# A list-scheduled attention, token mixer and gated unit: first scores without fillers ahead, leads and delays by kind of step, angles of batch 0 from group 20

## The chip, the cores and the metric

The kernel runs on one core of one Trainium2 chip. The metric is the device time of one execution in microseconds (us). Before the change the median of three runs is 404.01 us (402.75, 404.01 and 409.04).

## What is computed

The reference does three things one after the other, for 2 batches of 768 tokens, in float32. The first is local attention: 8 heads of 64 (four pairs of heads to a batch), each query against the keys less than 16 positions away and against 24 block summaries (the maximum of each 32 keys, the mean of each 32 values). The second mixes tokens with angles, the third is a gated unit.

```python
# attention, per head
scores_l = where(mask_l, scale * q @ k.T, -1e9)
scores_s = scale * q @ k_sum.T + log(32)
a = softmax(concat([scores_l, scores_s]))
x = concat over heads of a @ concat([v, v_sum])
# token mixer, d_model 512
theta = x @ w_theta
y = w_tok_r @ (x * cos(theta)) + w_tok_i @ (x * sin(theta))
u = x + y
x = u + max(u @ w_ch, 0)
# gated unit, d_ff 1024
h = gelu(x @ w_in); u, v = split(h)
v_n = (v - mean) / sqrt(var + 1e-6) * g_ln
out = x + (u * (w_sg @ v_n + b_sg)) @ w_out
```

## The kernel before

**How the order is made.** The kernel doesn't write its instructions in the order in which they run. Each step is recorded by `op` (L70) with a name, the engines it could run on with an estimated cost on each, what it reads and writes, and the buffers it needs. `Plan.run` (L93) then plays a list schedule through at build time: it gives each step a due time (its place in the recorded order of TensorE's work, handed back along the dependencies), and whenever an engine is free it takes the ready step that is due first, if its buffers are free. Where a step could run on several engines, the costs are weighed by `LOAD` (L260), a price for ScalarE (ACT), VectorE (DVE) and GpSimd (POOL) that changes at 90 us of the planned time. On TensorE (PE) a step of another `mode` than the last has to be due earlier by `STAY` (L258) to be taken. What comes out is a fixed order on each engine; on the chip each engine runs its list in that order and waits for what a step needs. The last loop of the builder (L1203 on) issues the list.

**Tiling.** Pairs of heads are numbered p = 0 to 7 (four to a batch), and each pair has four groups g = 4p to 4p+3: a half of the 768 tokens (`hf`) and a head (`h`). For the two groups of a half, `scores` (L609) first puts the mask into PSUM with two matmuls against an identity (`M`, L621, of `mask` and `id16`), adds the scores with 24 small matmuls (`S`, L631), takes the maximum on VectorE (`nb`, L642) and the exponentials on ScalarE (`exp`, L647). `turned` (L651) transposes a group on TensorE (`PT`), and copies it out (`Pt`); `values` (L662) multiplies with the values (`O`); `norm` (L684) divides and transposes back (`X`, L714) into `xT`. `prep_k` lays out a pair's keys in windows (`kv..<-k`, `kv..<-ks`) on any of the three elementwise engines, `prep_v` does the block means of the values (`vsp`, `vsg`), 129 columns (`VC`) to a window. Pair 0's loads are in `load_pair` (L410): keys, queries, `consts` (`craw`: identity and masks), values, one after the other in SyncE's (SP's) queue.

**The start.** L1056 records `warm`, 15 matmuls of 480 columns of the zeroed `mask` into a PSUM tile nobody reads (`fill`, L1044), which keep TensorE busy while pair 0 loads. From there on to `warm_end` the loop at L1203 puts more of them (fillers) on TensorE wherever the plan has an idle stretch of over 0.25 us ahead of a step.

**After the attention.** For each of the 12 token blocks n (6 to a batch) `theta` does 12 matmuls of 512 columns with the four weights `w_th`, on the parts `xs` of `xT`; `angles` (`ki`, `kk`, `ra`, `rb`) brings the angle into range, `rotated` takes sine and cosine (only after the last exponential) and makes `zs0` to `zs11` (`z`, `zh`, `zl`, two each). `y_big` uses them in 24 matmuls of 512 columns a block. A weight is loaded as 64-bit words and taken apart into a high and a low part (`weights`, L436: `.h`, three steps of bits on VectorE, `.hi`, `.lo`), and each product is three matmuls (`mm3`, L366 to L368). Then come `y_small`, `ch`, `in_v`, `in_u`, `sg` and `outp`.

`PLAN` says in which order pairs and weights are loaded (`want`), and after which group each block of batch 0 is recorded (`theta`); the loop at L1103 records the attention:

```python
    "theta": [26, 28, 30, 32, 34, 36],
...
        for n in range(NT):
            if PLAN["theta"][n] == s:
                x_parts(n)
                theta(n)
                angles(n)
```

## Time and profile before

| what | value |
|---|---|
| median of 3 runs | 404.01 us |
| the profiled execution's own time | 404.08 us |
| its span, first to last instruction | 402.3 us |
| TensorE busy | 394.3 us, 98% of the span |
| VectorE, ScalarE, GpSimd busy | 296.9, 181.7, 47.8 us |
| fillers on TensorE | 44 matmuls of 480 columns |
| read from and written to memory | 33.97 MB, 3.15 MB |

Busy time is a share of the span; a busy TensorE is one that has a matmul in flight, since matmuls overlap. The number of matmuls that begin in a stretch says more: 512 columns begin every 0.225 to 0.235 us where nothing holds them up. In the views a matmul of a small float32 tile may be counted as two. The chain of waits runs back from the last instruction to what released each step. Numbers such as L621 are lines of the kernel before; in the list of the changed kernel the same steps have other lines.

### The profile page before, as it was taken

What the parts mean: (1) busy time and instruction counts of PE and PEld (TensorE: products, weight loads), DVE (VectorE), ACT (ScalarE), POOL (GpSimd) and SP (SyncE); (2) the same over time, 40 slices, a digit from 0 to 9 for tenths busy, and PEclk for the clock granted to TensorE, in tenths of its full rate; (3) what the DMA queues carried; (4) which work ended last, traced back from release to release, by engine and by line L of the source; (5) the groups of instructions that cost most, each with busy time, mean ns of one, the idle gap of its engine ahead of it and who ended that gap; (6) DMA issues with size and microseconds to landing.
All of it is one profiled execution on the core that took longest, in us unless ns stands there. A gap on an engine that the chain in (4) does not pass through costs nothing.

```text
span 402.3 us, 7345 instructions
## 1 busy us (share of the span) xinstructions
PE 394.3 (98%) x2922; PEld 327.2 (81%) x2922; DVE 296.9 (74%) x578; ACT 181.7 (45%) x384; POOL 47.8 (12%) x75
## 2 busy tenths in 40 slices
PE   8999999999999999999999999999999999999996
PEld 3776677788876888889998989889889888898986
DVE  2789879989999996896999898856376523606732
ACT  3687788787769852341675425453000113520000
POOL 1347686323000000000000000000000000000000
PEclk9999999999999999999999999999999999999999
DMA  8999995020000002428950035000000210000012
GB/s 249 274 330 267 264 295 190 7 102 1 0 2 0 0 2 69 136 68 279 412 204 1 2 78 185 0 0 2 0 2 15 104 40 0 2 0 2 0 55 103
DMA packets 15826, 37.59 MB, mean 93 GB/s; under 512 B 1968, under 2 KB 4656, under 8 KB 15792
## 3 DMA queue, kind: packets, MB, share of 16 engines
q1 hardware_dynamic: 15792, 37.13, 29.3%
q8 instruction: 23, 0.38, 0.4%
q14 instruction: 11, 0.09, 0.1%
HBM read 33.97 MB, written 3.15 MB: 92 GB/s over the span
## 4 chain that ended last, share of the span: by engine, by line
PE 84%; DVE 10%; issue 2%; ACT 1%; DMA 1%; SPq 0%; DVEq 0%
PE y L366 7%; PE y L367 7%; PE y L368 7%; PE sg L367 4%; PE sg L368 4%; PE sg L366 4%; PE O L675 3%; PE S L631 3%; PE ch L368 3%; PE ch L366 3%; PE u L367 3%; PE u L368 3%; PE ch L367 3%; PE u L366 3%; PE o L366 3%; PE o L368 3%
## 5 line engine op out<-in xcount | busy, mean ns | idle before, releaser
L1016 DVE SCALAR_TENSOR_TENSOR gf<-sg,g_sb,bsg 128x512 f32<-128x512 f32 (+1 forms) x16 | 9.9, 616 | 25.1 <-PE sg L368 25.1
L647 ACT ACTIVATE P<-S,nb 128x120 f32<-128x120 f32 x96 | 26.9, 371 | 3.0 <-DVE nb L642 2.9
L367 PE MATMUL y<-w_ri,zs 128*128 128x256 f32 x96 | 27.1, 282 | 0.0
L366 PE MATMUL y<-w_ri,zs 128*128 128x256 f32 x96 | 27.1, 282 | 0.0
L368 PE MATMUL y<-w_ri,zs 128*128 128x256 f32 x96 | 27.1, 282 | 0.0
L354 ACT ACTIVATE x<-xT 128x256 fp32r<-128x256 f32 (+1 forms) x13 | 6.2, 497 | 41.3 <-PE o L368 33.7
L1037 DVE TENSOR_TENSOR ob<-o,xT 128x512 f32<-128x512 f32 (+1 forms) x16 | 8.9, 558 | 18.5 <-PE o L368 18.5
L368 PE MATMUL ch<-u,w_ch 128*128 128x256 f32 (+1 forms) x64 | 21.7, 339 | 0.0
L366 PE MATMUL ch<-u,w_ch 128*128 128x256 f32 (+1 forms) x64 | 21.7, 339 | 0.0
L368 PE MATMUL u<-x,w_inu 128*128 128x512 f32 (+1 forms) x64 | 21.6, 338 | 0.0
L367 PE MATMUL u<-x,w_inu 128*128 128x512 f32 (+1 forms) x64 | 21.6, 338 | 0.0
L367 PE MATMUL ch<-u,w_ch 128*128 128x256 f32 (+1 forms) x64 | 21.6, 338 | 0.0
L366 PE MATMUL u<-x,w_inu 128*128 128x512 f32 (+1 forms) x64 | 21.6, 337 | 0.0
L366 PE MATMUL o<-g,w_out 128*128 128x512 f32 (+1 forms) x64 | 21.5, 336 | 0.0
L367 PE MATMUL o<-g,w_out 128*128 128x512 f32 (+1 forms) x64 | 21.5, 336 | 0.0
L368 PE MATMUL o<-g,w_out 128*128 128x512 f32 (+1 forms) x64 | 21.5, 336 | 0.0
L954 DVE BATCH_NORM_STATS2 st<-vf 128x6 f32<-128x512 f32 x12 | 8.3, 692 | 16.3 <-ACT vf L951 16.3
L366 PE MATMUL th<-w_th,xs 128*128 128x512 f32 x48 | 20.0, 417 | 0.0
L366 PE MATMUL y<-w_r,zs 128*128 128x512 f32 x48 | 19.1, 399 | 0.6 <-ACT zs L354 0.4
L951 ACT ACTIVATE vf<-v 128x512 f32<-128x512 f32 x12 | 7.2, 598 | 27.8 <-PE v L368 27.7
L354 ACT ACTIVATE Pt<-PT 120x384 f32<-120x384 f32 x31 | 14.9, 491 | 10.0 <-PE PT L656 9.8
L368 PE MATMUL y<-w_r,zs 128*128 128x512 f32 x48 | 18.9, 394 | 0.5 <-DVE zs L384 0.5
(196 smaller groups left out, 1213.1 us busy)
## 6 DMA issues: line engine op xcount, KB each, us to landing
k<-in_kT_dram SPq DMA_DIRECT2D x8, 384.0 KB, 8.5
kv<-in_qT_dram SPq DMA_DIRECT2D x8, 384.0 KB, 9.6
w_r<-in_w_rT_dram SPq DMA_DIRECT2D x6, 512.0 KB, 7.6
w_i<-in_w_iT_dram SPq DMA_DIRECT2D x6, 512.0 KB, 6.2
kv<-in_vW_dram SPq DMA_DIRECT2D x8, 338.6 KB, 9.2
w_th<-in_w_theta_dram SPq DMA_DIRECT2D x4, 512.0 KB, 8.2
w_ch<-in_w_ch_dram SPq DMA_DIRECT2D x4, 512.0 KB, 6.7
w_inv<-in_w_in_dram SPq DMA_DIRECT2D x4, 512.0 KB, 7.4
```

Source lines behind the costliest of these rows:

```text
L354: e.activation(dst, src, AF.Copy, scale=scale)
L366: PE.matmul(ps, ah, bh, start=first, stop=False, skip_group_check=True)
L367: PE.matmul(ps, ah, bl, start=False, stop=False, skip_group_check=True)
L368: PE.matmul(ps, al, bh, start=False, stop=last, skip_group_check=True)
L631: PE.matmul(T(f"S{g}")[64 * ab:64 * ab + 64, t * WC:(t + 1) * WC], T(f"kv{p}_0")[r0, 64 * w:64 * w + 64], T(kv)[r0, c:c + WC], start=False ...
L647: ACT.activation(T(pt)[:, t * WC:(t + 1) * WC], T(ps)[:, t * WC:(t + 1) * WC], AF.Exp, bias=T(nb)[:, t:t + 1], scale=1.0),
L675: PE.matmul(T(ps)[64 * ab:64 * ab + 64, o:o + 65], T(sb)[:WC, t * P + 64 * ab:t * P + 64 * ab + 64], T(vv)[:WC, c:c + 65], start=True, sto ...
L951: op(f"vf{b}_{i}", {"ACT": 0.6}, lambda e: ACT.activation(T(vf)[:], T(ps)[:], AF.Gelu_apprx_tanh), [ps], [vf], table="gelu")
L954: op(f"bs{b}_{i}", {"DVE": 0.7}, lambda e: DVE.bn_stats(out=T(st)[:], in_=T(vf)[:]), [vf], [st])
L1016: lambda e: DVE.scalar_tensor_tensor(out=T(gf)[:, :n], in0=T(ps)[:, :n], scalar=g_sb[:, f:f + 1], in1=T("bsg")[:, o:o + n], op0=ALU.mult, ...
L1037: op(f"ob{b}_{half}_{c}", {"DVE": 0.15 + 0.53 * n / 512}, lambda e: DVE.tensor_tensor(out=T(ob)[:, :n], in0=T(ps)[:, :n], in1=xT[:, c, b * ...
```

## The change

The list gets another order. A table `BIAS` gives each kind of step (its name without digits) a lead or delay that is taken off its due time; `STAY` goes from 4.0 to 15.5; `LOAD` gets other prices and the second set from 80 us on; some estimated costs are corrected; `PLAN` records the angles of block 0 after group 20 and those of blocks 1 to 4 after groups 26 to 29, and loads pair 3 ahead of theta's weight 1, and pair 7 ahead of pair 6. At the start, 12 fillers run from a tile `zeros` of their own, and the loop puts none ahead of the first scores (it starts at `S0`). The mask is made in three steps (`mask0`, `mask1`, `mask2`, the last on VectorE or GpSimd), pair 0's queries are loaded in two halves with `craw` between them, and a window of the values has 130 columns. A second method, `latest`, could set due times from a played schedule and play again; with `ROUNDS = 1` it is played once.

```diff
-VC = 129
+VC = 130
...
-            o.due -= o.bias
+            o.due -= BIAS.get(o.kind, 0.0)
...
-STAY = 4.0
-LOAD = ({"ACT": 1.0, "DVE": 1.6, "POOL": 1.5}, {"ACT": 0.8, "DVE": 1.0, "POOL": 4.0}, 90.0)
+ROUNDS = 1
+BIAS = {
+    "M": 25, "PT": -2, "S": -1, "abs": 4, "ba_": -5, "blocks": 25, "bs_": 8, "bsg": -24,
...
+STAY = 15.5
+LOAD = ({"ACT": 0.71, "DVE": 1.34, "POOL": 0.92}, {"ACT": 0.08, "DVE": 1.79, "POOL": 23.66},
+        80.0)
...
-    "want": [("pair", 0), ("pair", 1), ("th", 0), ("pair", 2), ("th", 1), ("pair", 3),
-             ("th", 2), ("th", 3), ("pair", 4), ("r", 0), ("pair", 5), ("i", 0),
-             ("pair", 6), ("pair", 7), ("r", 1), ("i", 1)],
+    "want": [("pair", 0), ("pair", 1), ("th", 0), ("pair", 2), ("pair", 3), ("th", 1), ("pair", 4),
+             ("th", 3), ("th", 2), ("pair", 5), ("r", 0), ("i", 0), ("pair", 7), ("pair", 6),
+             ("i", 1), ("r", 1)],
...
-    "theta": [26, 28, 30, 32, 34, 36],
+    "theta": [20, 26, 27, 28, 29, 36],
...
+            load("q0_0", lambda: T("kv0_0")[:, :S // 2], qT[b, r][:, :S // 2], [("q", p, 0)])
             buf("craw", "t")
             load("craw", lambda: T("craw")[:, :P + 3 * WC], consts, ["craw"])
+            load("q0_1", lambda: T("kv0_0")[:, S // 2:S], qT[b, r][:, S // 2:], [("q", p, 1)])
...
-    op("zeros", {"DVE": 0.3}, lambda e: DVE.memset(mask[:], 0.0), [], ["mask"])
+    buf("zeros", "t")
+    op("zeros", {"DVE": 0.3}, lambda e: DVE.memset(
+        T("zeros")[:, :64 + 2 * WC].bitcast(BF16), 0.0), [], ["zeros"])
+    op("mask", {"DVE": 0.3}, lambda e: DVE.memset(mask[:], 0.0), [], ["mask"])
-    op("warm", {"PE": 4.5}, lambda e: fill(15), ["mask"], ["wps"])
+    op("warm", {"PE": 4.5}, lambda e: fill(12, T("zeros")[:].bitcast(BF16)), ["zeros"], ["wps"])
...
-    op("masks", {"DVE": 0.9}, masks, ["craw"], ["mask"], port=True)
+    op("mask0", {"DVE": 0.2}, masks(0), ["craw", "mask"], ["mask0"], port=True)
+    op("mask1", {"DVE": 0.25}, masks(1), ["craw", "mask0"], ["mask"], port=True)
+    op("mask2", {"DVE": 0.2, "POOL": 0.3}, masks(2), ["craw", "mask"], ["mask2"], port=True)
...
-            filling = (filling or o.name == "warm") and o.name != "warm_end"
+            filling = (filling or o.name == "S0") and o.name != "warm_end"
```

The matmuls are the same in number and shape, but for 44 fillers that become 21 and the 130th column of the values. VectorE has 542 instructions for 578, ScalarE 408 for 384 less its 7 table loads, GpSimd 81 for 75: copies of high parts (16 of `g`, 5 of `vn`, 4 each of `zs` and `u`) go from VectorE to ScalarE, and layouts of keys from ScalarE to GpSimd.

How the order on the engines changes is shown at three places. The first is TensorE's list at the first scores, where `wps` is the tile of the fillers, `id16` the identity and `S0` to `S3` are the PSUM tiles of the first four groups. Before:

```order
L1047 LDWEIGHTS mask_68
L1047 MATMUL wps_92<-mask_68 128x480
L621 LDWEIGHTS id16_67
L621 MATMUL S0_190<-mask_68,id16_67 128x360
L621 LDWEIGHTS id16_67
L621 MATMUL S1_192<-mask_68,id16_67 128x360
L621 LDWEIGHTS id16_67
L621 MATMUL S2_194<-mask_68,id16_67 128x360
L621 LDWEIGHTS id16_67
L621 MATMUL S3_196<-mask_68,id16_67 128x360
L631 MATMUL S0_190<-kv0_1_156,kv0_0_81 64x120
L631 MATMUL S1_192<-kv0_1_156,kv0_0_81 64x120
```

And after:

```order
L1128 LDWEIGHTS zeros_88
L1128 MATMUL wps_102<-zeros_88 128x480
L702 LDWEIGHTS id16_67
L702 MATMUL S0_173<-mask_68,id16_67 128x360
L702 LDWEIGHTS id16_67
L702 MATMUL S1_175<-mask_68,id16_67 128x360
L702 LDWEIGHTS id16_67
L702 MATMUL S2_177<-mask_68,id16_67 128x360
L702 LDWEIGHTS id16_67
L702 MATMUL S3_179<-mask_68,id16_67 128x360
L712 MATMUL S0_173<-kv0_1_156,kv0_0_81 64x120
L712 MATMUL S1_175<-kv0_1_156,kv0_0_81 64x120
```

Before, the row shown of a filler is the last of 30 ahead of the first mask matmul, 15 of `warm` and 15 put in by the loop; after, it is the last of 12. Further on, the scores of groups 2 and 3 follow at once on those of 0 and 1, where before the block means of pair 0 stood between them.

The second place is TensorE's list after the scores of group 20, from the transpose of group 18 on; `th0` is the PSUM tile of theta's block 0, `xs0` its input, and 443 to 445 are the lines of `mm3`. Before:

```order
L656 MATMUL PT18_1010<-ident_66,P18_990 120x128 x3
L1047 LDWEIGHTS mask_68
L1047 MATMUL wps_92<-mask_68 128x480
L578 MATMUL vsp5_1022<-kv5_2_263,blocks_69 32x129 x2
L578 MATMUL vsp5_1022<-kv5_3_331,blocks_69 32x129 x2
L578 MATMUL vsp5_1022<-kv5_2_263,blocks_69 32x129
L578 MATMUL vsp5_1022<-kv5_3_331,blocks_69 32x129 x3
L578 MATMUL vsp5_1022<-kv5_2_263,blocks_69 32x129
L578 MATMUL vsp5_1022<-kv5_3_331,blocks_69 32x129 x2
L578 MATMUL vsp5_1022<-kv5_0_163,blocks_69 32x129
L714 MATMUL X4_0_1043<-ident_66,x1_0_1020 128x128 x3
L656 MATMUL PT19_1050<-ident_66,P19_1008 120x128 x3
```

And after:

```order
L737 MATMUL PT18_995<-ident_66,P18_959 120x128 x3
L795 MATMUL X4_0_1004<-ident_66,x1_0_993 128x128 x3
L443 MATMUL th0_1012<-w_th0_487,xs0_887 128x512
L444 MATMUL th0_1012<-w_th0_487,xs0_887 128x512
L445 MATMUL th0_1012<-w_th0_487,xs0_887 128x512
L443 MATMUL th0_1012<-w_th1_648,xs0_887 128x512
L444 MATMUL th0_1012<-w_th1_648,xs0_887 128x512
L445 MATMUL th0_1012<-w_th1_648,xs0_887 128x512
L737 MATMUL PT19_1027<-ident_66,P19_985 120x128 x3
L1128 LDWEIGHTS id16_67
L1128 MATMUL wps_102<-mask_68,id16_67 128x480
L443 MATMUL th0_1012<-w_th2_928,xs0_887 128x512
```

A filler stood after the transpose of group 18; now two weights' worth of theta's block 0 follows there, and the other two come soon after. Before, block 0 came after the scores of group 26.

The third is SyncE's queue of loads around pairs 6 and 7. Before:

```order
L395 DMA w_i0_378<-in_w_iT_dram 128x512
L395 DMA k6_398<-in_kT_dram 128x768
L395 DMA kv6_0_401<-in_qT_dram 128x768
L395 DMA kv6_2_481<-in_vW_dram 96x516
L395 DMA kv6_3_541<-in_vW_dram 96x903
L395 DMA kv6_0_401<-in_vW_dram 96x129
L395 DMA k7_566<-in_kT_dram 128x768
L395 DMA kv7_0_568<-in_qT_dram 128x768
```

And after:

```order
L472 DMA w_r0_327<-in_w_rT_dram 128x512
L472 DMA w_i0_374<-in_w_iT_dram 128x512
L472 DMA k7_398<-in_kT_dram 128x768
L472 DMA kv7_0_400<-in_qT_dram 128x768
L472 DMA kv7_2_473<-in_vW_dram 96x520
L472 DMA kv7_3_483<-in_vW_dram 96x910
L472 DMA kv7_0_400<-in_vW_dram 96x130
L472 DMA k6_577<-in_kT_dram 128x768
```

The five loads of pair 7 now stand ahead of the first of pair 6.

## Rows read from the trace of the kernel before

**Rows 1.** The page, part 1: busy time, share and instructions of an engine.

```profile
PE 394.3 (98%) x2922; PEld 327.2 (81%) x2922; DVE 296.9 (74%) x578; ACT 181.7 (45%) x384; POOL 47.8 (12%) x75
```

**Rows 2.** Stretches: length, busy us (xcount) per engine, PEclk, DMA share, GB/s.

```profile
10.00:20.00 10.00, 10.00 (x168) 7.74 (x167) 7.17 (x15) 6.22 (x20) 3.90 (x9) 1.00 1.05 273
20.00:30.00 10.00, 9.68 (x175) 7.22 (x175) 8.87 (x23) 8.37 (x25) 4.30 (x9) 1.00 1.04 328
40.00:50.00 10.00, 9.13 (x156) 6.63 (x148) 8.19 (x17) 7.06 (x24) 6.65 (x13) 1.00 1.05 263
120.00:130.00 10.00, 9.37 (x38) 6.90 (x38) 10.00 (x18) 9.97 (x20) 0.00 (x0) 1.00 0.00 0
130.00:140.00 10.00, 9.61 (x40) 7.62 (x41) 9.93 (x18) 9.39 (x17) 0.00 (x0) 1.00 0.00 0
140.00:160.00 20.00, 20.00 (x89) 16.36 (x88) 16.66 (x30) 7.83 (x13) 0.00 (x0) 1.00 0.06 21
360.00:402.30 42.30, 39.00 (x228) 34.25 (x226) 21.05 (x40) 0.00 (x0) 0.00 (x0) 0.99 0.11 38
```

**Rows 3.** Timeline of the start: start us, us, engine, line, op, out<-in [idle before].

```profile
1.17 5.15 PE L1047 MATMUL wps<-mask 128*128 128x480 bf16 x15 [1.17 <-DVE mask L1054]
...
3.81 0.94 ACT L354 ACTIVATE kv<-k 128x672 f32<-128x672 f32 x2 [1.80 <-DMA k<-in_kT_dram]
...
6.44 0.31 ACT L354 ACTIVATE ident<-craw 128x128 f32<-128x128 f32 x1 [1.28 <-DMA craw<-in_consts_dram]
...
7.07 3.20 PE L1047 MATMUL wps<-mask 128*128 128x480 bf16 x15 [0.75 <-DVE mask L1085]
...
9.97 0.94 ACT L354 ACTIVATE kv<-k 128x672 f32<-128x672 f32 x2 [2.91 <-DMA k<-in_kT_dram]
...
10.10 0.77 PE L621 MATMUL S<-mask,id 128*128 128x360 bf16 x4
```

**Rows 4.** DMA issues: out<-in, queue, xcount, KB each, median us to landing.

```profile
k<-in_kT_dram SPq DMA_DIRECT2D x8, 384.0 KB, 8.5
craw<-in_consts_dram SPq DMA_DIRECT2D x1, 244.0 KB, 4.8
```

**Rows 5.** Chain of waits in order of time: start us, us, what.

```profile
11.65 2.75 PE vsp L578 x24
...
34.09 1.12 PE wps L1047 x5
43.90 0.87 issue
...
98.06 1.20 DVE zs L384 x2
```

**Rows 6.** Timeline of TensorE where y begins and where it waits.

```profile
111.55 0.39 PE L366 MATMUL y<-w_r,zs 128*128 128x512 f32 x1
...
129.11 0.50 PE L366 MATMUL y<-w_r,zs 128*128 128x512 f32 x1 [0.41 <-ACT zs L354]
...
130.30 0.50 PE L368 MATMUL y<-w_r,zs 128*128 128x512 f32 x1 [0.46 <-DVE zs L384]
```

**Rows 7.** Timeline of TensorE and of SyncE's queue, around pair 6.

```profile
43.01 0.35 SPq L395 DMA_DIRECT2D k<-in_kT_dram  x1
...
61.08 0.85 PE L631 MATMUL S<-kv,kv 64*64 64x120 f32 x24
```

**Rows 8.** Groups by line and shape, VectorE, 10 to 70 us: busy us, mean ns.

```profile
L463 DVE SCALAR_TENSOR_TENSOR cw_th<-w_th,cw_th 128x512 int32<-128x512 int32 x4 | 3.7, 918 | 0.0
```

**Rows 9.** Groups by line and shape, all engines, whole run.

```profile
L463 DVE SCALAR_TENSOR_TENSOR cw_i<-w_i,cw_i 128x512 int32<-128x512 int32 x6 | 4.2, 692 | 0.2
L356 POOL TENSOR_SCALAR kv<-k 128x672 f32<-128x672 f32 x3 | 2.3, 754 | 2.5 <-DMA k<-in_kT_dram 1.4 <-PE PT L656 1.0
L384 POOL TENSOR_TENSOR xs<-xT,xs 128x512 fp32r<-128x512 f32 x5 | 6.5, 1312 | 0.2
```

**Rows 10.** Waits of SyncE's queue: us, times, longest.

```profile
SPq L395 <- PE O L675: 27.3, 6, 13.4
```

More of the change, by code (lines that the diff above doesn't have):

```diff
@@ L70, in op @@
     def op(self, name, eng, fn, r=(), w=(), table=None, lat=None, port=False, dma=0.0,
-           after=(), bias=0.0, mode="full"):
+           after=(), mode="full"):
         o = Op(n=len(self.ops), name=name, eng=eng, fn=fn, reads=r, writes=w, table=table,
-               lat=lat, port=port, dma=dma, deps=set(), succ=set(), bufs=set(), bias=bias,
-               mode=mode)
+               lat=lat, port=port, dma=dma, deps=set(), succ=set(), bufs=set(), mode=mode,
+               kind="".join(c for c in name if not c.isdigit()))
         for k in r:
@@ L99, in run @@
                 d.succ.add(o)
-            for b in o.bufs:
-                first.setdefault(b, o.n)
-                uses[b] = uses.get(b, 0) + 1
-        order = {}
-        for b in sorted(first, key=lambda b: (first[b], b)):
-            order.setdefault(self.kind[b], []).append(b)
         t = 0.0
@@ L116, in run @@
                 o.due = min(o.due, s.due - cost(o) - 0.15)
-            o.due -= o.bias
+            o.due -= BIAS.get(o.kind, 0.0)
+        best = None
+        for j in range(ROUNDS):
+            try:
+                done = self.play()
+            except RuntimeError:
+                if best is None:
+                    raise
+                break
+            if TRACE:
+                print("round", j, self.total)
+            if best is None or self.total < best[0]:
+                best = (self.total, done, {o.n: (o.at, o.end, o.on, o.due) for o in ops},
+                        dict(self.slot))
+            self.latest(done)
@@ new lines, in run, with latest @@
+        self.total, done, was, self.slot = best
+        for o in ops:
+            o.at, o.end, o.on, o.due = was[o.n]
+        return done
+    def latest(self, done):
+        free = {}
+        home = {}
+        end = max(o.end for o in done)
+        last_in = {}
+        for o in done:
+            for b in o.bufs:
+                last_in.setdefault(self.slot[b], []).append((b, o))
+        after = {}
+        for lst in last_in.values():
+            names = []
+            for b, o in lst:
+                if not names or names[-1][0] != b:
+                    if any(x[0] == b for x in names):
+                        names[[x[0] for x in names].index(b)][1].append(o)
+                        continue
+                    names.append((b, [o]))
+                else:
+                    names[-1][1].append(o)
+            for (_, xs), (_, ys) in zip(names, names[1:]):
+                for x in xs:
+                    after.setdefault(x.n, []).append(ys[0])
+        for o in reversed(done):
+            d = (o.end - o.at) if not o.dma else o.eng["SP"]
+            lat = o.lat if o.lat is not None else (0.0 if o.dma else self.LAT[o.on])
+            x = end
+            for s in (*o.succ, *after.get(o.n, ())):
+                x = min(x, s.due - (0.0 if s.on == o.on and not o.dma else lat)
+                        - ((o.end - o.at - d) if o.dma else 0.0))
+            x = min(x, free.get(o.on, end))
+            o.due = x - d
+            free[o.on] = o.due
@@ L118, in run, with play @@
+    def play(self):
+        ops = self.ops
+        first, uses = {}, {}
+        for o in ops:
+            for b in o.bufs:
+                first.setdefault(b, o.n)
+                uses[b] = uses.get(b, 0) + 1
+        order = {}
+        for b in sorted(first, key=lambda b: (first[b], b)):
+            order.setdefault(self.kind[b], []).append(b)
         free_at = {e: 0.0 for e in ("PE", "DVE", "ACT", "POOL", "SP")}
-        dma_at = 1.9
+        dma_at = 0.9
         slots = {k: [(0.0, f"{k}{j}") for j in range(n)] for k, n in self.homes.items()}
@@ L582, in prep_v @@
         buf(f"vsp{p}", "ps")
-        op(f"vsp{p}", {"PE": 2.7 if one else 0.7}, sums,
+        op(f"vsp{p}", {"PE": 2.8 if one else 0.8}, sums,
            ["blocks", *(("v", p, j) for j in range(3))], [f"vsp{p}"], mode="VS")
@@ L636, in scores @@
         ss = [f"S{g}" for g in gs]
[L637 to L639 removed]
+        op(f"M{gs[0]}", {"PE": 0.32}, masks, ["id16", "mask", *["mask2"] * hf], ss)
+        op(f"S{gs[0]}", {"PE": 0.7}, mm,
+           [("q", p, hf), *((x, p, j) for j in js for x in ("k", "ks"))], ss, mode="S")
         for g in gs:
@@ L1079, with masks, f @@
             want_y(c, [x])
-    def masks(e):
-        m = mask[:].rearrange("p (i c) -> p i c", c=WC)[:, :, :WK]
-        c = T("craw")[:, P:P + 3 * WC].rearrange("p (i c) -> p i c", c=WC)[:, :, :WK]
-        for i0, n, j in ((0, 1, 0), (1, 2, 1), (3, 1, 2)):
-            DVE.tensor_copy(m[:, i0:i0 + n], c[:, j:j + 1].to_broadcast([P, n, WK]))
+    def masks(j):
+        def f(e):
+            m = mask[:].rearrange("p (i c) -> p i c", c=WC)[:, :, :WK]
+            c = T("craw")[:, P:P + 3 * WC].rearrange("p (i c) -> p i c", c=WC)[:, :, :WK]
+            i0, n = ((0, 1), (1, 2), (3, 1))[j]
+            copy(e, m[:, i0:i0 + n], c[:, j:j + 1].to_broadcast([P, n, WK]))
+        return f
     def which(e):
```

48 lines of the change are left out of this document (31 added, 17 removed).

## The prediction

> **What bounds the kernel now.** I read the page first, then the stretches, then the timelines of the start and of the stage of y, and last the chain of waits and the groups by line. The page gives TensorE 394.3 us busy, 98% of the span [rows 1]; no other engine comes above 74%. So time can be won in three ways only: TensorE's first useful matmul begins earlier, it does fewer matmuls that nobody reads, or its holes close. The stretches say where holes are [rows 2]. From 10 to 20 us there is none; from 20 to 30 TensorE is idle for 0.32 us, from 40 to 50 for 0.87. In the stage of y, 140 to 160 us shows the full pace: 89 matmuls in 20 us, or 0.225 us for one. From 120 to 130 only 38 begin and from 130 to 140 only 40, where 44.5 would fit: 6.5 + 4.5 = 11 missing, 11 x 0.225 = 2.5 us. The timeline shows what they wait for: a matmul of y after 0.41 us for ScalarE's `zs`, another after 0.46 us for VectorE's [rows 6]; VectorE has 10.00 and 9.93 us of work in these two stretches. The granted clock is 1.00 in all of them, and 0.99 in the last.
>
> At the start [rows 3] the keys of pair 0 are there at 3.81 (ScalarE begins on them), `craw` at 6.44, and the mask is done when the second fifteen fillers begin, at 7.07, which waited for it. The mask matmuls M wait for nothing but those fillers, 3.20 us of them, and begin at 10.10. From there to the end the kernel is one stream of TensorE.
>
> **Part 1, the head: -3.75 us.** The loop's 15 fillers ahead of M go. What is late next is `craw`. Between the landing of the keys and that of `craw`, 2.63 us passed for the queries (as large as the keys, 384 KB) and `craw` itself, 244 KB [rows 3, 4]; now half of the queries stand ahead, 192 KB. In proportion 2.63 x 436/628 = 1.83, so `craw` lands at 3.81 + 1.83 = 5.64. Mask and identity took 7.07 - 6.44 = 0.63 us; they are cut finer but are the same work, and with 0.08 for a step on another engine M begins at 6.35. Gain 10.10 - 6.35 = 3.75. Bounds: if `craw` lands no earlier, M begins at 7.15 and 2.95 are won. If it lands earlier still, the 12 warm fillers set M: 15 took 5.15 us, and three of them at the later pace of 3.20/15 = 0.21 cost 0.64, so 12 end 4.5 us after a start that a second memset of 0.3 us (the plan's number) puts at 1.47, at 5.97; then 4.15 are won. Behind M come the scores of four groups in place of two, and then the block means, which need the values. Those landed after 6.44 and before the next keys, 9.97 [rows 3]; 594 of 978 KB stand for the values, so about 6.44 + 3.53 x 594/978 = 8.58. Half the queries stand behind `craw` now, so their bytes are in front of the values as before. The block means are asked for at 6.35 + 0.77 (four M) + 2 x 0.75 (two scores) = 8.62. That is close; at the latest bound it costs 9.97 - 8.62 = 1.35, which would leave 2.4 of the gain. I take nothing, since the row by size is nearest. The scores of pair 1 come 2.75 us of block means [rows 5], 0.8 of transposes and 0.4 of masks later, at 12.6, and its keys, there at 9.97, need 0.94 (ScalarE) or 0.75 + 0.3 (GpSimd, [rows 9]) of layout: no wait.
>
> **Part 2, the later fillers: -1.0 us.** 14 stood behind the first scores, 9 stand there now. Five took 1.12 us in the chain [rows 5], 0.21 to 0.22 each: 5 x 0.21 = 1.0. If each covers a true wait it is 0 that is won.
>
> **Part 3, the stage of y: -1.8 us.** In the new list TensorE meets `zs3_0` after 144 matmuls of theta and 138 of y, where it stood after 144 and 72; `zs9_0` after 162 of y for 114. VectorE has 223 instructions up to `zs3_0` for 218, and 229 for 234 up to `zs9_0`. So TensorE comes 66 x 0.225 = 14.9 us later at `zs3_0`, and VectorE, at 10 us for 18 instructions [rows 2], 2.8 us later. Those waits should go. Against it stands `zs0`: y begins after 108 matmuls of theta for 144, 36 x 0.225 = 8.1 us earlier, and it was done at 98.06 + 1.20 = 99.26, while y began at 111.55 [rows 5, 6]. Now y begins at 111.55 - 8.1 - 4.75 = 98.7. If VectorE is as much earlier as TensorE is, `zs0` is done at 94.5 + 2.8 = 97.3; if it isn't, at 102.1, a wait of 3.4. Of the 2.5 us I take 1.8 as won (ends: 0 and 2.5).
>
> **Part 4, the attention: +0.3 us.** Theta's block 0 moves ahead of pair 5's last groups: work that TensorE had to do anyway, put where it waits. What could be late is its inputs, and pair 6. Pair 6 is now loaded after pair 7, so its keys take the place in the queue that pair 7's had, issued at 43.01 [rows 7]; they land 8.5 us on in the median [rows 4], at 51.5, and the layout costs up to five steps on GpSimd (0.75 for the windows, 1.31 for a low part of `xs` in front of it, [rows 9]), some 5 us: ready at 56.5. The scores of group 24 began at 61.08 [rows 7]; less 4.75, plus 12 matmuls of theta that now stand ahead (2.7), they are asked for at 59.0. Slack 2.5. DMA is busy all that time (share 1.04 to 1.05, [rows 2]), so a queue that slips is felt here. For a small wait at one of these places or at `zs0` I put 0.3; bounds -1.2 (all idle time of 20 to 50 us closes too) and +3.4 (`zs0` as above).
>
> From 140 us on no hole is seen, the matmuls are the same, and the last stretch ends with 39.0 busy of 42.3 us, of which the store behind the last matmul is the same. VectorE gives 36 instructions away and ScalarE takes 31 there and elsewhere; ScalarE is the least busy of the two (181.7 against 296.9). I take 0. The 130th column and the split of the mask: 0, beside work of other engines.
>
> What GpSimd takes on deserves a second look. VectorE's second step of a theta weight, which reads two operands from SBUF, takes 918 ns in the stretch in which GpSimd works, and 692 ns for the same step of `w_i`, in most of which GpSimd rests [rows 8, 9]. So each collision costs about 0.2 us of VectorE. The Trainium skill (SBUF — State Buffer, "Who interferes with whom") says that such an instruction and a GpSimd one that reads SBUF keep each other out through a shared port; the trace agrees with it. By that rule the change, with 81 GpSimd instructions for 75 and theta's parts earlier among them, has more of this in the attention, which speaks for the second rival.
>
> The sum: 404.08 (the profiled execution; 0.07 over the median, which I leave) - 3.75 - 1.0 - 1.8 + 0.3 = 397.8 us.
>
> **The rivals.**
> - *All waits go.* The head gains 4.15, y the whole 2.5, and the 1.2 us of idle time in 20 to 50 us close: 404.08 - 4.15 - 1.0 - 2.5 - 1.2 = 395.2. For it speaks that ScalarE and VectorE now get y's inputs long before; against it, that the attention's waits are on ScalarE and GpSimd, to which the list gives more.
> - *TensorE only waits elsewhere.* The fillers covered true waits (0 for part 2), the y waits move to `zs0` (0 for part 3), and the values come 0.5 late: 404.08 - 3.25 + 0.3 = 401.1. For it: ScalarE and GpSimd are busiest just there, 7 to 8.4 and 4 to 6.7 us in 10 [rows 2]. Against it: a filler runs only where the plan, not the chip, sees a wait.
> - *The change does not do what it says at the head*: `craw` lands as before, since the 16 engines move both transfers at once. 397.8 + 0.8 = 398.6, inside the forecast.
> - *Pair 6 comes too late: slower.* SyncE's queue holds each load until its buffer is free, and waited six times for a values matmul, 13.4 us at the longest [rows 10]. If the keys of pair 6 get that wait at their new place, they are issued at 56.4, laid out at 69.9, and group 24 waits 10.9 us: 408.7. It decides from an issue later than 43.0 + 2.5 = 45.5 on, one for one, and is slower than before from 51.7 on. Against it: in the trace the load at that place was issued without such a wait.
>
> **How the numbers follow.** Forecast (396 to 400.5): 0.56, of which 0.12 for the third rival, the smaller gain at the head. All waits go: 0.20. TensorE waits elsewhere: 0.17. Pair 6 late: 0.07. The range goes from a little beyond the better rival, 394.5, to 402.2, beyond the second. 2% of 404.01, about what a measurement of this kernel can tell from no change, is 8.1: faster means below 395.9. That is nearly all of the better rival and a little of the forecast's edge: 0.20. Slower means above 412.1, the far end of pair 6's: 0.03. Within: 0.77.
>
> **What would show it.** Right: M begins near 6.35 without a filler of the loop ahead; 89 matmuls to 20 us all through y; `zs` no longer among TensorE's releasers there. Wrong: M still at 7.1 (part 1's bound); idle TensorE behind `vsp` of pair 0, released by the values; idle time of over 1 us ahead of theta's first block, of group 24's scores (released by `kv`), or of the first y (by `zs`); a granted clock under that of [rows 2] with the fillers gone, for which the trace of before gives no price.

## The result and the profile after

The changed kernel takes 400.12 us in the median of 10 executions (396.31 to 406.72), the kernel before 404.69 us (402.45 to 410.29, 10 executions beside it). The ratio is 0.9878, with a 95% interval of 0.9843 to 0.9914: about 4.9 us less (404.08 x 0.0122), between 3.5 and 6.3. The forecast was 6.3 us less, 397.8; its range, 394.5 to 402.2, holds the result. It is within 2%, which was given 0.77. The forecast's 6.3 us is the far end of the measured interval. Executions of one kernel differ by over 1% here; the ratios leave out those more than 1.5% above the quickest of their kernel, but not all in which the granted clock falls for a stretch.

The profiled execution took 399.96 us, its span is 398.2. The page, busy time of the engines first, then the chain that ended last by engine:

```profile
PE 388.1 (97%) x2899; PEld 324.9 (82%) x2899; DVE 282.5 (71%) x542; ACT 199.6 (50%) x415; POOL 49.0 (12%) x81
...
PE 86%; DMA 9%; DVE 3%; SPq 1%; ACT 1%; issue 0%; DVEq 0%
```

TensorE is 6.2 us less busy than in [rows 1], but the span is only 4.1 us shorter: it waits more. And 9% of the chain is DMA. In the kernel before that line reads:

```profile
PE 84%; DVE 10%; issue 2%; ACT 1%; DMA 1%; SPq 0%; DVEq 0%
```

The stretches of after that answer to [rows 2]:

```profile
10.00:20.00 10.00, 9.00 (x141) 6.81 (x140) 7.24 (x16) 6.96 (x23) 5.64 (x12) 1.00 1.05 290
20.00:30.00 10.00, 9.40 (x174) 6.88 (x172) 6.66 (x16) 8.45 (x24) 6.50 (x12) 1.00 1.05 282
40.00:50.00 10.00, 9.05 (x153) 6.71 (x153) 9.44 (x24) 8.63 (x26) 8.36 (x13) 1.00 1.04 287
120.00:130.00 10.00, 10.00 (x46) 8.23 (x45) 9.79 (x18) 9.84 (x18) 0.00 (x0) 1.00 0.00 1
130.00:140.00 10.00, 10.00 (x45) 8.19 (x44) 9.90 (x18) 9.71 (x18) 0.00 (x0) 1.00 0.00 0
140.00:160.00 20.00, 20.00 (x89) 16.29 (x88) 17.38 (x31) 7.28 (x12) 0.00 (x0) 1.00 0.17 53
```

The stage of y is full now, 46 and 45 matmuls where 38 and 40 began. The attention isn't: from 10 to 20 us, without a hole before, 1.0 us is missing; from 20 to 30, 0.60 for 0.32. The start, as in [rows 3], with the waits for the values of pair 0 (a weight load, PEld, at 9.85) and of pair 1 (at 14.88):

```profile
1.49 4.98 PE L1128 MATMUL wps<-zeros 128*128 128x480 bf16 x12 [1.49 <-DVE zeros L1137]
...
6.59 0.31 ACT L431 ACTIVATE ident<-craw 128x128 f32<-128x128 f32 x1 [1.53 <-DMA craw<-in_consts_dram]
...
7.19 0.77 PE L702 MATMUL S<-mask,id 128*128 128x360 bf16 x4 [0.72 <-DVE mask L438]
...
9.85 2.12 PEld L659 LDWEIGHTS vsp<-kv,blocks 96*24 96x24 f32 x20 [0.22 <-DMA kv<-in_vW_dram]
...
14.88 0.86 PE L659 MATMUL vsp<-kv,blocks 96*32 96x130 f32 x20 [0.40 <-DMA kv<-in_vW_dram]
```

And two marks further on, from TensorE's timeline: the first matmul of y, and the last output.

```profile
101.88 0.39 PE L443 MATMUL y<-w_r,zs 128*128 128x512 f32 x1
...
394.65 0.28 PE L445 MATMUL o<-g,w_out 128*128 128x256 f32 x1
```

In the kernel before the last output begins at 398.72. With these marks the time divides into three. The changed kernel starts y with 36 matmuls of theta still to do, 36 x 0.225 = 8.1 us, which are counted to the middle part here.

| part | before | after | difference | foretold |
|---|---|---|---|---|
| to the first mask matmul | 10.10 | 7.19 | -2.91 | -3.75 |
| from there to y, with all of theta | 111.55 - 10.10 = 101.45 | 101.88 - 7.19 + 8.1 = 102.79 | +1.34 | -1.0 + 0.3 = -0.7 |
| from y to the last output | 398.72 - 111.55 = 287.17 | 394.65 - 101.88 - 8.1 = 284.67 | -2.50 | -1.8 |
| sum | 398.72 | 394.65 | -4.07 | -6.25 |

So in these two executions the middle part is what went wrong. There five fillers (1.0 us) went, and yet it is 1.3 us longer: the attention waits some 2.3 us more. It is one execution of each; the last table of the experiments shows how far the middle part moves between executions. The view of waits, TensorE's from 8 us on and VectorE's from 10 on, up to 60 us (us in total, times, longest):

```profile
PE X L795 <- DVE x L783: 3.8, 5, 0.9
...
DVE ks L614 <- DMA k<-in_kT_dram: 3.1, 4, 1.4
DVE cw_th L541 <- POOL w_th L554: 3.1, 2, 1.7
```

The kernel before has for VectorE's wait on keys, in the same stretch:

```profile
DVE ks L533 <- DMA k<-in_kT_dram: 0.2, 1, 0.2
```

TensorE waits for normalised blocks `x`, five times; and VectorE, which makes them, waits for keys, 3.1 us for 0.2, and as long for theta's weights (`cw_th`), for which it did not wait there before. How late keys become a wait for `x` is seen on the two engines' timelines:

```profile
51.66 0.95 DVE L614 TENSOR_REDUCE ks<-k 128x24 f32<-128x768 f32 x1 [1.42 <-DMA k<-in_kT_dram]
...
52.95 0.56 DVE L783 TENSOR_TENSOR x<-O,ri 128x384 f32<-128x384 f32 x1
...
53.56 0.55 PE L795 MATMUL X<-ident,x 128*128 128x128 f32 x3 [0.91 <-DVE x L783]
```

VectorE runs its list in order. The maxima of a new pair's keys (`ks`) stand ahead of the division by the sums (`ri`, `ri`, `x`); the keys are 1.42 us late, and everything behind them with them. The other four X have three different causes:

```profile
16.94 0.43 DVE L541 TENSOR_SCALAR cw_th<-w_th 128x512 int32<-128x512 int32 x1 [1.72 <-POOL w_th L554]
...
18.32 0.55 PE L795 MATMUL X<-ident,x 128*128 128x128 f32 x3 [0.60 <-DVE x L783]
...
23.11 0.95 DVE L614 TENSOR_REDUCE ks<-k 128x24 f32<-128x768 f32 x1 [1.18 <-DMA k<-in_kT_dram]
...
26.23 0.52 PE L795 MATMUL X<-ident,x 128*128 128x128 f32 x3 [0.52 <-DVE x L783]
...
29.09 0.43 DVE L541 TENSOR_SCALAR cw_th<-w_th 128x512 int32<-128x512 int32 x1 [1.37 <-POOL w_th L554]
...
31.73 0.52 PE L795 MATMUL X<-ident,x 128*128 128x128 f32 x3 [0.83 <-DVE x L783]
...
41.03 0.55 PE L795 MATMUL X<-ident,x 128*128 128x128 f32 x3 [0.95 <-DVE x L783]
```

The X at 26.23 stands behind late keys as well. Those at 18.32 and 31.73 stand behind the first bit step of a theta weight, which waited for GpSimd's copy of a weight that GpSimd had itself waited for. Ahead of the one at 41.03 VectorE has no wait; there a step of 1.93 us, begun at 35.95, is what is long (see "GpSimd beside VectorE"). The chain of waits has these causes too: loads of keys, and between them, from 29.75 to 42.20, work of VectorE and ScalarE with that step in it:

```profile
21.67 8.05 DMA k<-in_kT_dram
...
36.03 1.86 DVE cw_th L541
...
42.20 9.37 DMA k<-in_kT_dram
```

### The profile page after: what moved, and what is told of

It reads as the page before. It is cut to its first block, busy times and chain, and to the rows that moved or that the text cites. A ratio compares the mean times of both kernels' runs of the same rounds, so it can differ in the third digit from the quotient of the medians.

```text
span 398.2 us, 7273 instructions
## 1 busy us (share of the span) xinstructions
PE 388.1 (97%) x2899; PEld 324.9 (82%) x2899; DVE 282.5 (71%) x542; ACT 199.6 (50%) x415; POOL 49.0 (12%) x81
## 4 chain that ended last, share of the span: by engine, by line
PE 86%; DMA 9%; DVE 3%; SPq 1%; ACT 1%; issue 0%; DVEq 0%
PE y L444 8%; PE y L443 8%; PE y L445 8%; DMA k<-in_kT_dram 4%; PE sg L445 4%; PE sg L444 4%; PE sg L443 4%; PE th L443 3%; PE ch L445 3%; PE ch L443 3%; PE o L445 3%; PE ch L444 3%; PE o L444 3%; PE o L443 3%; PE u L445 3%; PE u L444 3%
## 5 line engine op out<-in xcount | busy, mean ns | idle before, releaser
L431 ACT ACTIVATE g<-gf 128x512 fp32r<-128x512 f32 (+1 forms) x16 | 8.4, 525 | 59.7 <-DVE gf L1100 59.7
L443 PE MATMUL ch<-u,w_ch 128*128 128x512 f32 (+1 forms) x64 | 21.7, 338 | 0.0
L445 PE MATMUL ch<-u,w_ch 128*128 128x512 f32 (+1 forms) x64 | 21.6, 338 | 0.0
L444 PE MATMUL ch<-u,w_ch 128*128 128x512 f32 (+1 forms) x64 | 21.6, 337 | 0.0
L443 PE MATMUL th<-w_th,xs 128*128 128x512 f32 x48 | 20.3, 424 | 0.0
L445 PE MATMUL sg<-w_sg,vn 128*128 128x512 f32 x48 | 19.0, 397 | 0.0
L444 PE MATMUL sg<-w_sg,vn 128*128 128x512 f32 x48 | 19.0, 395 | 0.0
L443 PE MATMUL sg<-w_sg,vn 128*128 128x512 f32 x48 | 18.9, 393 | 0.0
L444 PE MATMUL y<-w_i,zs 128*128 128x512 f32 x48 | 18.8, 392 | 0.0
L445 PE MATMUL th<-w_th,xs 128*128 128x512 f32 x48 | 18.8, 392 | 0.0
L444 PE MATMUL y<-w_r,zs 128*128 128x512 f32 x48 | 18.8, 392 | 0.0
```

Of the source, the lines that this page charges most:

```text
L431: e.activation(dst, src, AF.Copy, scale=scale)
L443: PE.matmul(ps, ah, bh, start=first, stop=False, skip_group_check=True)
L444: PE.matmul(ps, ah, bl, start=False, stop=False, skip_group_check=True)
L445: PE.matmul(ps, al, bh, start=False, stop=last, skip_group_check=True)
```

## The experiments

**The head alone.** In the kernel before, the loop begins at `S0`:

```diff
-            filling = (filling or o.name == "warm") and o.name != "warm_end"
+            filling = (filling or o.name == "S0") and o.name != "warm_end"
```

> The kernel before, with only the loop's start moved: it puts no filler ahead of the first scores, all else as before. If the head is worth what it saves (theory A), the first mask matmul begins at about 7.15 us for 10.10 and the time falls by 2 to 3 us, to about 401.5. If the loads and layouts set the pace of the attention (theory B), TensorE waits more between 10 and 60 us: its idle time there, 1.46 us before, grows by 2 or more, and the time falls by less than 1 us.

Ratio 0.995 (0.9909 to 0.9992), 2.0 us less. In the profiled execution the first mask matmul is at 7.42 and TensorE is idle for 0.17 us from 10 to 60 us: theory A. But this execution took 399.5 us, where the median of the ten is 403.9, and the ratio's interval, 0.3 to 3.7 us less, leaves room for both theories. It is the one with the quickest loads of all that were profiled:

```profile
10.00:50.00 40.00, 39.83 (x689) 29.13 (x687) 36.71 (x79) 31.14 (x97) 25.91 (x44) 1.00 1.05 302
```

**The head put back.** The changed kernel with 15 warm fillers more:

```diff
-fill(12, T("zeros")[:].bitcast(BF16))
+fill(27, T("zeros")[:].bitcast(BF16))
```

> The changed kernel with 27 warm fillers for 12, so that the first mask matmul begins at about 9.7 us (1.49 + 4.98 + 15 x 0.213) for 7.19; nothing else moves. Theory A (the waits of the attention come from the order of TensorE's and VectorE's lists): idle time from 10 to 60 us stays at 4 to 4.6 us, and the time is 2.2 to 2.7 us over that of the changed kernel. Theory B (loads and layouts set the pace): the waits shrink to 2 or less and the time is at most 1 us over it.

Ratio 0.9937 (0.989 to 0.9984), 2.4 us over the changed kernel's, as theory A has it (the two intervals overlap), though the mask matmul began at 8.61, only 1.42 later than in the changed kernel's profile. The idle time from 10 to 60 us rose to 5.6 us (10 - 7.99 in the row below, and 40 - 36.42 from 10 to 50). In this execution a later start doesn't make the waits go. And something new stands here, a clock of 0.83 in the stretch with the longest wait, X at 52.35 for 1.91 us:

```profile
10.00:50.00 40.00, 36.42 (x642) 27.23 (x635) 32.69 (x69) 29.13 (x88) 26.53 (x46) 1.00 1.05 281
50.00:60.00 10.00, 7.99 (x76) 5.72 (x74) 7.97 (x15) 6.03 (x19) 6.94 (x9) 0.83 0.87 246
```

**X later.** In the list that the changed kernel issues, each X moves, and the fillers stay with the steps that they stood ahead of (the lines for that are left out):

```diff
     done = plan.run()
...
+    for x in [o for o in done if o.kind.startswith("X")]:
+        i = done.index(x)
+        done.remove(x)
+        pe = [j for j in range(i, len(done)) if done[j].on == "PE"][:2]
+        rd = min(done.index(s) for s in x.succ)
+        done.insert(min(pe[1] + 1, rd), x)
...
```

> The changed kernel with each transposition X of a normalised block moved behind the next two steps of TensorE's list (or up to the copy that reads it); fillers and the other lists as they are. If the attention's new waits are there only because X stands too close behind its normalisation (theory A), the five waits of X, 3.8 us together, fall under 1.5 us and the time falls by 1.5 to 3 us against the changed kernel. If TensorE waits for what VectorE and the loads supply anyway (theory B), the waits move to the matmuls of values and scores, and the time changes by less than 0.7 us.

Ratio 0.9892 (0.9834 to 0.995) from only four executions: no gain is shown. The waits moved, as theory B has it. Its profiled execution had `craw` as late as 7.63 us and is read for the places of the waits alone: with X out of the way, the mask matmuls and the values wait.

```profile
PE S L702 <- DVE x L783: 2.7, 2, 1.4
PE O L756 <- POOL kv L433: 2.1, 1, 2.1
PE X L795 <- DVE x L783: 0.6, 1, 0.6
```

**`craw` first.** In the same list `craw` moves ahead of both halves of the queries:

```diff
     done = plan.run()
+    at = {o.name: o for o in done}
+    done.remove(at["craw"])
+    done.insert(done.index(at["q0_0"]), at["craw"])
```

> The changed kernel with craw loaded straight behind the keys, ahead of both halves of the queries; all other lists are the same. If loads land one after the other by their bytes (the prediction's reading), craw lands at about 4.8 us, the mask matmul is set by the warm fillers and begins at about 6.5 for 7.19, and the time falls by 0.7 us. If the queues move several loads at once, so that a load's place among four early ones hardly sets its landing, craw lands at 6.2 or later and the start moves by less than 0.4 us.

The mask is begun at 4.83 and the mask matmul at 6.27, so `craw` does land earlier with no queries ahead of it. Yet the ratio is 0.994 (0.9903 to 0.9977), no better than the changed kernel's 0.9878: over ten executions a start 0.9 us earlier bought nothing. The profiled one did keep it: y begins at 100.89 for 101.88, the last output at 393.67 for 394.65. But six of the ten have a mean clock under 0.998, two of the changed kernel's first ten; what that costs here isn't shown apart.

```profile
4.83 0.37 DVE L438 CAST mask<-craw 128x96 bf16<-128x96 f32 x2
...
6.27 1.05 PE L702 MATMUL S<-mask,id 128*128 128x360 bf16 x4
```

**Who closed the holes of y.** Two experiments: the changed kernel with the old prices of the second set,

```diff
-LOAD = ({"ACT": 0.71, "DVE": 1.34, "POOL": 0.92}, {"ACT": 0.08, "DVE": 1.79, "POOL": 23.66}, 80.0)
+LOAD = ({"ACT": 0.71, "DVE": 1.34, "POOL": 0.92}, {"ACT": 0.8, "DVE": 1.0, "POOL": 4.0}, 80.0)
```

> The changed kernel with the prices of the second set of LOAD as before (ACT 0.8, DVE 1.0, POOL 4.0): up to 80 us all lists are the same; TensorE still meets zs3_0 after 145 matmuls of y, but 23 copies go back from ScalarE to VectorE. If the holes in y went because TensorE asks later (theory A, the prediction's), none comes back and the time is that of the changed kernel within 0.7 us. If they went because ScalarE took the copies (theory B), VectorE is late again, 5 to 11 matmuls are missing between 100 and 140 us, and the time is 1 to 2.5 us over the changed kernel's.

and the kernel before with the new ones:

```diff
-LOAD = ({"ACT": 1.0, "DVE": 1.6, "POOL": 1.5}, {"ACT": 0.8, "DVE": 1.0, "POOL": 4.0}, 90.0)
+LOAD = ({"ACT": 1.0, "DVE": 1.6, "POOL": 1.5}, {"ACT": 0.08, "DVE": 1.79, "POOL": 23.66}, 80.0)
```

> The kernel before with the changed prices of the second set of LOAD (ACT 0.08, DVE 1.79, POOL 23.66, from 80 us on): TensorE's list keeps its order (zs3_0 met after 144 of theta and 73 of y), but ScalarE takes 36 copies more. Theory A (TensorE's order closes y): the two holes at zs, 0.4 and 0.46 us, and most of the 11 missing matmuls stay, time within 1 us of before. Theory B (ScalarE's copies do): no matmul is missing from 110 to 150 us, and the time falls by 2 to 2.5 us.

The stage of y of the first:

```profile
120.00:130.00 10.00, 10.00 (x46) 8.29 (x45) 9.90 (x18) 9.84 (x19) 0.00 (x0) 1.00 0.00 0
```

And of the second:

```profile
120.00:130.00 10.00, 10.00 (x45) 8.18 (x44) 9.93 (x18) 9.87 (x18) 0.00 (x0) 1.00 0.00 0
```

Both are full. Each of the two means is enough by itself: TensorE asking later, or ScalarE taking copies. The second has ratio 0.9933 (0.99 to 0.9967), 2.7 us, what the 2.5 us of holes are worth; from the first y, at 109.50, to its last output, at 394.40, it takes 284.9 us, for 287.2. The first has 0.9946 (0.9907 to 0.9986), more time than the changed kernel's, although no hole came back and its profiled span, 397.5, is shorter; five of its ten executions have a mean clock under 0.998, with a median of 403.7 us against 400.6 of the other five, so that its higher median goes with the clock; why the clock fell more often isn't settled here.

**GpSimd beside VectorE.** The four low parts of theta's weights go to VectorE:

```diff
     done = plan.run()
+    for o in done:
+        if o.name.startswith("w_th") and o.name.endswith(".lo"):
+            o.on = "DVE"
```

> The changed kernel with the four low parts of theta's weights made on VectorE in place of GpSimd, at the same places of the lists. In the changed kernel VectorE's first bit step of a theta weight takes 803 ns in the mean from 10 to 70 us, and the second 897. If VectorE is held up by GpSimd's work beside it and that makes the norms, and so X, late (theory A): the first step falls to 0.5 us or less, the second under 0.75, and the waits of X around 31.7 and 41.0 us (0.83 + 0.95) shrink by 0.8 or more together; time 0.5 to 1.5 us under the changed kernel's. If the collisions hide (theory B), VectorE only gets 4 x 0.68 = 2.7 us more work: X waits longer by 0.5 or more, and the time is 0 to 1.5 us over it.

Groups by line and shape, VectorE from 10 to 70 us (busy us, mean ns), of the changed kernel:

```profile
L544 DVE SCALAR_TENSOR_TENSOR cw_th<-w_th,cw_th 128x512 int32<-128x512 int32 x4 | 3.6, 897 | 0.0
...
L541 DVE TENSOR_SCALAR cw_th<-w_th 128x512 int32<-128x512 int32 x4 | 3.2, 803 | 3.1 <-POOL w_th L554 3.1
```

And of this one:

```profile
L544 DVE SCALAR_TENSOR_TENSOR cw_th<-w_th,cw_th 128x512 int32<-128x512 int32 x4 | 2.8, 704 | 0.0
...
L541 DVE TENSOR_SCALAR cw_th<-w_th 128x512 int32<-128x512 int32 x4 | 2.1, 520 | 5.0 <-POOL w_th L554 5.0
```

The steps fall as foretold, 803 to 520 and 897 to 704 ns: 4 x 0.28 + 4 x 0.19 = 1.9 us of VectorE were collisions. One of them in the changed kernel, with GpSimd's two instructions beside it:

```profile
35.69 1.26 POOL L461 TENSOR_TENSOR w_th<-cw_th,w_th 128x512 fp32r<-128x512 f32 x1
...
35.95 1.93 DVE L541 TENSOR_SCALAR cw_th<-w_th 128x512 int32<-128x512 int32 x1
...
36.93 0.67 POOL L554 TENSOR_SCALAR w_th<-w_th 128x512 f32<-128x512 f32 x1
```

VectorE's step, 0.42 us elsewhere, ends at 37.88, 0.28 us behind GpSimd's second one. The Trainium skill (SBUF — State Buffer, "Who interferes with whom") has it that whoever issues first holds the shared port for its whole instruction; the trace agrees, 1.93 for 0.42 us. With the low parts on VectorE, the X that waited 0.95 us at 41.03 waits 0.27. Six profiled executions of the changed list, of its variants and of this one bear it out: that X waits 0.95, 0.95 and 0.74 us in the three in which the step took 1.93, 1.95 and 1.44, and 0.27 us and twice not at all in the three in which it took 0.81, 0.96 and 0.42 (the execution with fillers ahead of this X is left out). So the collision does cost TensorE a wait. But the time doesn't follow: ratio 0.9929 (0.9873 to 0.9984), and all waits for X together are as long as before, 4.1 us in five waits from 8 to 60 us for 3.8. VectorE also waits for keys (3.3 us) and for weights (5.0). This execution had the slowest loads of its family in the last table (276 GB/s) and a clock of 0.83 from 30 to 40 us, and eight of the ten have a mean clock under 0.998, so what the collisions cost in time stays open.

**The order of loads.** The changed kernel with the `want` of before:

```diff
-    "want": [("pair", 0), ("pair", 1), ("th", 0), ("pair", 2), ("pair", 3), ("th", 1), ("pair", 4),
...
+    "want": [("pair", 0), ("pair", 1), ("th", 0), ("pair", 2), ("th", 1), ("pair", 3),
...
```

> The changed kernel with the order of loads of before (theta's weight 1 ahead of pair 3, pair 6 ahead of pair 7); the list is played again with it, but TensorE begins as early and meets y as in the changed kernel. If the attention's early start needs the pairs' loads early (theory B), keys come late: idle time from 10 to 60 us, 4.6 in the changed kernel, grows by 2 us or more, and the time is 2 us or more over the changed kernel's. If the order of loads doesn't bind (theory A), both stay within 1 us.

Ratio 0.9915 (0.9872 to 0.9958), idle from 10 to 60 us 4.57 us for 4.63. The idle time doesn't grow, as theory A has it, and no worth of the order of loads is shown. X waits once, 0.7 us; the values' matmuls wait for ScalarE instead, 2.2 us.

**The changed kernel again, and with fillers in the waits.** The first is the same file. The second:

```diff
         if o.on == "PE":
...
+            if o.name in ("X0_0", "X1_0", "X1_1", "X2_1", "X4_0"):
+                fill(3)
```

> The changed kernel once more, on the chip of the next three, so that they can be held against it directly: 4 to 6 us under before. Where craw lands, 6.6 us in its first profile, should differ by up to 1 us from run to run (theory: the loads' landing varies), or stay within 0.2 us of it (theory: the order of the loads fixes it).

> The changed kernel with three fillers (0.64 us) ahead of each of the five X that waited 0.5 to 0.95 us for a norm; nothing else moves. If idle gaps in the attention cost TensorE its clock in some executions (theory C), fewer runs show a mean clock under 0.998, no stretch of the profile shows under 0.95, and the median falls by 0.5 to 2 us against the changed kernel's. If the clock has nothing to do with those gaps (theory D), the share of such runs stays, and the time is the same or up to 1 us longer, since not all of the fillers lie in a wait.

The same list gave 0.9891 (0.983 to 0.9951), with `craw` at 6.19 for 6.59 and two stretches in which the clock falls, after waits of 1.20 and 1.00 us at 30.3 and 31.9, and of 1.88 us at 54.75:

```profile
30.00:40.00 10.00, 8.70 (x126) 6.34 (x130) 8.40 (x19) 5.87 (x19) 6.93 (x13) 0.83 1.04 301
...
50.00:60.00 10.00, 8.12 (x77) 6.09 (x76) 6.82 (x15) 5.49 (x18) 6.71 (x11) 0.83 0.80 219
```

There matmuls of theta begin 0.43 us apart where they take 0.23, the lower of TensorE's two clocks (1.2 for 2.4 GHz):

```profile
55.91 0.43 PE th L445
...
59.05 0.24 PE th L444
```

A stretch of 10 us at 0.83 has 10 x 0.17 = 1.7 us less of TensorE's clock. With fillers in the waits the clock is 1.00 in every stretch of the profile, as it was in the changed kernel's first; 2 of its 12 executions had a mean clock under 0.998, against 6 of 16 of the changed kernel and 11 of 79 of the kernel before. That points to theory C, but 2 of 12 and 6 of 16 are too few to tell apart. Its ratio is 0.9905 (0.9868 to 0.9941): no time is won, as theory D has it. The clock does go with the time: the changed kernel's six executions under 0.998 have a median of 402.7 us, its other ten 399.2.

**The parts without the table.** The kernel before with the loop's start and the prices changed as above, and then also with 12 warm fillers and `craw` ahead of the queries:

> The kernel before with two edits only: the loop's fillers begin at S0 (no filler of the loop ahead of the first scores), and the second set of LOAD is the changed one. By themselves these gave 0.995 and 0.9933. If the change's gain is the head and the stage of y (theory A), the two add to about 0.988, the changed kernel's own ratio, without its table of leads and its order of loads and angles. If the table and the new order matter as well (theory E), it stays at 0.992 or above.

> The same with craw loaded ahead of the queries and 12 warm fillers for 15, so that the mask isn't held by them: craw lands at about 4.9 us (as in the experiment with craw first), the first mask matmul begins at about 6.4 us for 7.4. If an earlier head is worth what it saves (theory A), 0.5 to 1 us under the one before it, and at or under the changed kernel. If the attention takes it back in waits (theory B), no difference, or more runs with a lower clock.

The first gave no interval: its executions ran from 396.8 to 406.6 us, but for one of 2160.9. The one of 396.8 had a mean clock of 0.999, the four others of the range 0.991 to 0.996. The second is the sharper one. Its mask matmul begins at 5.82, 4.3 us earlier than before, and from y to the last output it takes 400.17 - 115.28 = 284.89 us, without the holes: 6.6 us should be won. The ratio is 0.9976 (0.9937 to 1.0016): nothing is, clear of noise. The chain of waits shows where the profiled execution lost it:

```profile
5.18 8.77 DMA kv<-in_vW_dram
13.96 10.17 DMA w_th<-in_w_theta_dram
24.15 11.87 DMA k<-in_kT_dram
...
39.71 11.29 DMA k<-in_kT_dram
```

Of its first 51 us these four loads are 42.1. In this execution the early start only makes the waits for keys, values and weights longer, as theory B has it. The clock falls too, by 10 x 0.07 + 10 x 0.10 = 1.7 us:

```profile
30.00:40.00 10.00, 7.42 (x116) 4.90 (x109) 6.07 (x14) 4.95 (x14) 4.06 (x8) 0.93 1.04 274
40.00:50.00 10.00, 10.00 (x158) 7.10 (x159) 6.63 (x15) 7.58 (x25) 4.57 (x9) 0.90 0.98 252
```

Eight of the twelve executions have a mean clock under 0.998, median 405.0 us; the four others have a median of 401.9, where the kernel before, beside them and at such a clock, has 403.6. So even at the full clock most of the 6.6 us doesn't arrive. No version here beats the changed kernel.

**All executions together.** The list from the first mask matmul to y is nearly one in each of the two families below, but for what the rows name. The rate is what DMA moved from 10 to 50 us (GB/s of that stretch; the share of the DMA engines is 1.03 to 1.05 in all), the attention is the time from the first mask matmul to y, with the 36 matmuls of theta counted as above. The next column takes off what stretches of 10 us with a clock under 1.00 lost.

| execution | first mask matmul | rate | attention | without the clock's loss | y begins, theta done |
|---|---|---|---|---|---|
| changed, old prices | 7.10 | 297 | 102.0 | 102.0 | 109.1 |
| changed, again | 6.79 | 293 | 106.0 | 102.6 | 112.8 |
| changed, `craw` first | 6.27 | 291 | 102.7 | 102.7 | 109.0 |
| changed | 7.19 | 289 | 102.8 | 102.8 | 110.0 |
| changed, fillers in waits | 7.23 | 284 | 105.8 | 105.8 | 113.0 |
| changed, 27 warm fillers | 8.61 | 281 | 104.7 | 103.0 | 113.3 |
| changed, low parts on VectorE | 7.15 | 276 | 107.1 | 105.4 | 114.2 |
| before, head alone | 7.42 | 302 | 99.6 | 99.6 | 107.0 |
| before, new prices | 9.78 | 296 | 99.7 | 99.7 | 109.5 |
| before | 10.10 | 284 | 101.5 | 101.5 | 111.6 |
| before, three edits | 5.82 | 275 | 109.5 | 107.8 | 115.3 |

In both families the attention tends to grow as the rate falls, but by how much depends on what is held beside it. Five executions of the changed list have nothing added between the mask matmul and y (old prices, again, `craw` first, changed, 27 warm fillers). Without the clock's loss their attention takes 102.0 to 103.0 us, in the order of their rates, although they start anywhere from 6.27 to 8.61: among them an earlier start is kept. The two others of that family have 15 fillers more, or four more steps on VectorE. In the family of the kernel before the slowest attention by far belongs to the lowest rate and to the earliest start, and which of the two makes it slow can't be told from one execution. The reverse, that the engines hold up the loads by freeing buffers late, is not what the queue shows: from 10 to 50 us SyncE waits for another engine for 1.1 us in the changed kernel and 1.6 in the kernel before, and for 7.5 in the execution with the quickest loads, the head alone. From y on, all of the changed family that were profiled take 292.8 to 293.0 us, so what differs between executions of one list lies ahead of y.

## Why the prediction was right, and where it was not

- **What bounds the kernel.** That "the kernel is one stream of TensorE" was taken from the trace of before, where it held. It holds from y on. Up to 50 us the DMA engines are as full as TensorE: their share was 1.04 to 1.05 in [rows 2], and those rows were used only as a warning for pair 6. An earlier start can run into this bound, as in the last experiment; it need not, as the head alone showed with quick loads and 0.17 us of idle time.
- **Part 1, -3.75; measured -2.91.** The step that failed is "in proportion 2.63 x 436/628". The third rival came true, and at its price of 0.8. `craw` landed at 6.59, and in all eight profiled executions with half of the queries ahead of it at 6.05 to 7.63, 6.55 in the mean; with the whole of them ahead, at 5.71 to 7.45 in four, 6.41 in the mean. Half of a load saved nothing that these twelve show, while no load ahead saved 1.7 us. From `craw` to M it took 7.19 - 6.59 = 0.60 us for the 0.71 assumed. The wait for pair 0's values, bounded at 1.35 and taken at nothing, is 0.22 us of a weight load; the 0.40 at 14.88 is for pair 1's, which the sum didn't have.
- **Part 2, -1.0.** The five fillers are gone as foretold; that they cost time before isn't shown apart. That none "covers a true wait" was wrong in one thing: what takes their place is waits in which the clock may fall.
- **Part 3, -1.8; measured -2.50**, its far end. No wait at `zs0` came. The reason given was enough, but so was another that the prediction didn't count: ScalarE's copies close the holes with TensorE's order unchanged.
- **Part 4, +0.3; measured some +2.3, in one execution of each.** Mechanism and place were wrong. Theta's first block waited only behind an X, group 24 not at all, so that the rival on pair 6 fell. The prediction asked when keys are laid out and scores wanted; it didn't ask what stands behind `ks` in VectorE's list. There stands the normalisation, and late keys stop it, and so do late weights and a step held up beside GpSimd: of the five X that wait, two stand behind keys, two behind weights, one behind that step. The bound of -1.2 to +3.4 held it.
- **The rivals.** "TensorE only waits elsewhere" is half of what happened: in the attention it does, in y it doesn't. "All waits go", 395.2, is what the quickest of the ten comes near, 396.31; it wasn't profiled, so whether quick loads made it isn't shown.
- **GpSimd.** The collisions are there, 1.9 us of VectorE, with 0.19 us for a second step where 0.2 was read from the rows, and speak for the second rival as the prediction has it: the longest stands on the chain of waits, and the X behind it waits 0.95 us. In a kernel's time no run shows their price.
- **Luck.** In the profiled pair the 0.7 us more in y nearly make up for the 0.8 less at the head, so that the miss of 6.25 - 4.07 = 2.2 us is nearly the attention's alone. The total held because errors of both signs met in a range 7.7 us wide.

Open is why DMA's rate differs by some 7% between executions of nearly one list, with its engines busy in all of them; how much of the gain of an early start the loads take back over many executions, and how much the clock; why half a load of queries takes as long as the whole to let `craw` pass; and whether `ks` behind the normalisation in VectorE's list, or fewer weights loaded ahead of 50 us, would give the head back. The last two were not tried.

## What to carry to other kernels

Before an engine is made to start earlier, ask what runs beside it at full share: a stream of transfers that keeps its engines full can take the gain back in some executions, and in the quickest one it doesn't show. On an engine that runs its list in order, an instruction that waits for a load holds up all behind it, so the price of a late load is read from that list, not from the one that uses the load. Before two medians are compared, count in how many executions of each the granted clock fell. When one list gives spans that differ by a hundredth, cut the span at marks and find the part in which they differ before a term is believed.
